# Attention and two feed-forward layers on one core: v's block sums on four quarters of TensorE's columns

## The chip, the cores and the metric

One core of a Trainium2 chip runs the whole kernel in one launch. Its engines are TensorE (matmul, PE in the profile, with its weight loads as PEld), VectorE (DVE), ScalarE (ACT), GpSimd (POOL) and SyncE (SP, which here issues every DMA). The metric is device time in microseconds of one execution; the median of several is compared.

## The reference, cut to what matters

```
# q, k, v: (2, 8, 768, 64) f32;  block 32, window 16
nb      = S // block                                   # 24 blocks
k_sum   = k.reshape(B, H, nb, block, D).max(axis=3)
v_sum   = v.reshape(B, H, nb, block, D).mean(axis=3)   # the sums that the change touches
scores  = [q k^T / 8 where |i - j| < 16 else -1e9,  q k_sum^T / 8 + log(32)]
a       = softmax(scores)                              # over 768 + 24 columns
attn    = a @ concat([v, v_sum])
x       = attn as (1536, 512)
h       = x @ w_in;  x = (h * cos(h)) @ w_out          # first feed-forward layer, 512 -> 2048 -> 512
...                                                    # second layer, solu and layer norm
```

## The kernel before

**Attention.** The 16 heads are taken as 8 pairs (n = 0 to 7), and the 768 queries of a pair as 12 tiles of 64, four tiles to a group, so three groups (g = 0, 1, 2) to a pair and 24 groups G. A query tile needs a window of 96 keys and the 24 block rows, 120 columns together. All engines follow one order written out by hand: `for step in range(29)` at the end of `attention()`. In a step TensorE makes the scores of group step+1 (`emit_s`, L561, tile `sps`), the transposes of the weights of group step-4 (`emit_t`, L598, `aps`) and the product with v of group step-5 (`emit_av`, L613, `ops`); where g is 2 it transposes k and q of pair n+2 (`emit_k` L494, `emit_q` L533). VectorE takes maxima and sums (L572, L585), GpSimd subtracts the maximum and multiplies by the reciprocal (L576, L591), ScalarE does the exponential (L581) and copies out of PSUM (`emit_kx`, `emit_kx_ends` with lines 522 and 525, `emit_qx` L547).

**v of a pair.** `load_v(n)` fills one of four buffers `vt` with the twelve overlapping windows: for each head one DMA of 240 KB (L440) and one of 48 KB (L444), in rows of 256 bytes. `sum_v(n)` (L472, tile `vsum`) sums blocks of 32 rows on TensorE: for each of twelve tiles one f32 matmul (two entries each in the trace) whose weights are 96 rows by 64 columns of ones and zeros from `strip`; tiles 0 to 5 add up in PSUM partitions 0 to 63 and tiles 6 to 11 in 64 to 127. `scale_v(n)` (L480) divides on ScalarE into `vm`. `place_vsum(n)` (L487) copies the 24 means behind the windows of all twelve tiles: two DMAs, each from 12 partitions of `vm` to 12 partitions of `vt`, every row written twelve times. The dictionaries `VSUM_AT` and `VLOAD_AT` say in which step pair n is summed and loaded; its placing is issued at the head of the step after its sum, and a load near the end of its step. `emit_av` of a pair's first group, in step 3n+5, needs the placed means.

**SP's order.** SP issues everything in the order of the program: loads of k and q (L408), of v, the placing, and the weights of the first layer (L141, tile `raw`, 512 KB each, eight in attention at the steps of `WSTEPS`). A weight tile then passes ScalarE (L162, L163), VectorE (L169), ScalarE and GpSimd (L186, L187).

**Fill.** The first four steps of the first layer (48 matmuls of 128x512, L277) are laid into attention's later steps: `FILL` says how many in which step. The first twelve add up in the one bank of pool `ps_h0`, which the sums of pairs 0 to 5 use before; the others need the banks of `ps_qk`, which are given over at step `QK_DONE`. Sums of pairs 6 and 7 stand in a `ps_qk` tile, between the k and q of two pairs. From the end of attention on, the two layers run (L277, L319, later L907, L1074).

```
VSUM_AT  = {1: 0, 5: 1, 8: 2, 10: 3, 13: 4, 14: 5, 16: 6, 19: 7}
VLOAD_AT = {1: 1, 4: 2, 6: 3, 8: 4, 10: 5, 13: 6, 16: 7}
```

Of the kernel before, what the change touches and what calls it, by code (L numbers as in the profile page):

```python
# [7 lines left out]
F32 = mybir.dt.float32  # L8
# [11 lines left out]
BAND = 16  # L20
QT = 64
WIN = 96
# [12 lines left out]
def fused_kernel(  # L35
# [15 lines left out]
    P = 128  # L51
    B, H, S, D = q.shape
# [4 lines left out]
    NT = S // QT  # L57
    NS = S // BLOCK
# [39 lines left out]
    DVE_X = 19  # L98
    DVE_NORM = 99
    LAST = 5  # L100
    QK_DONE = 20
    REBIAS = float(2.0 ** -112)
    NEGATIVE = float(2.0 ** 32)
    TOP3 = float(0.936 * 2.0 ** -29)
# [165 lines left out]
    def h_products(step):  # L270
        fg, tb, f = work[step]
        h = h_of[step] = h_tile(step)
        m = 0
        for c in range(KC):
            for (a, b_) in PASSES:
                w = weights.done[w1[fg][0][c]]
                nc.tensor.matmul(  # L277
                    h, lhsT=w[:, a, f * P:(f + 1) * P], rhs=xs_of[tb, c][:, b_, :],
                    start=(m == 0), stop=(m == 3 * KC - 1))
                m += 1  # L280
                yield
# [54 lines left out]
    ps_h0 = ps_stack.enter_context(tc.tile_pool(name="ps_h0", bufs=1, space=PSUM))  # L336
    qk_stack = ps_stack.enter_context(ExitStack())
    ps_qk = qk_stack.enter_context(tc.tile_pool(name="ps_qk", bufs=1, space=PSUM))
# [3 lines left out]
    def warm_up(n):  # L342

        if not n:
            return
        idle = idles[0]
        t = ps_h0.tile([P, 512], F32, tag="h", name="idle")
        for _ in range(n):
            nc.tensor.matmul(t, lhsT=idle[:, 0:P], rhs=idle, start=True, stop=True)


    FILL = {15: 3, 16: 3, 17: 3, 18: 3, 20: 4, 21: 4, 22: 4, 23: 4, 24: 4, 25: 4, 26: 4, 27: 4, 28: 4}
    early = (x for step in range(GF) for x in h_products(step))

    def fill(step):

        if step == QK_DONE:
            qk_stack.close()
            ps_h[0] = ps_stack.enter_context(tc.tile_pool(name="ps_h", bufs=3, space=PSUM))
        for _ in range(FILL.get(step, 0)):  # L360
            next(early, None)
# [23 lines left out]
    def attention():  # L385
        st = ExitStack()
        with st:
            io = st.enter_context(tc.tile_pool(name="io", bufs=2))
            fix = st.enter_context(tc.tile_pool(name="fix", bufs=1))
# [10 lines left out]
            q_t, k_t, v_t, kx_t, vs_t, qk_t, ks_t = {}, {}, {}, {}, {}, {}, {}  # L400
# [46 lines left out]
                    )  # L447
                v_t[n] = t

            HALF = NT // 2  # L450
            FIRST, FINAL, MID = 0, D, 2 * D
            strip = fix.tile([P, 3 * D + 2 * HALF], F32, name="strip")

            def block_columns():

                for at, row in ((FIRST, 0), (FINAL + 2 * HALF - 2, WIN - QT), (MID + 2 * HALF, BAND)):
                    nc.vector.tensor_reduce(
                        out=strip[:, at:at + 2],
                        in_=ident[:, row:row + QT].rearrange("p (b k) -> p b k", k=BLOCK), op=ALU.add, axis=AX.X)

            def blocks_of(t):
                at = FIRST if t == 0 else FINAL if t == NT - 1 else MID + 2 * HALF - 2 * (t % HALF)
                return strip[0:WIN, at:at + D]

            def sum_v(n):

                o = (ps_h0 if n < 6 else ps_qk).tile(
                    [P, 512] if n < 6 else [P, 2, 2, S // 2], F32, tag="h" if n < 6 else "qk", name="vsum")
                o = (o if n < 6 else o[:, 0, 0])[:, 0:P]
                for t in range(HALF):  # L470
                    for c in range(2):
                        nc.tensor.matmul(  # L472
                            o[D * c:D * c + D], lhsT=blocks_of(HALF * c + t),
                            rhs=v_t[n][0:WIN, HALF * c + t].rearrange("p j d -> p (j d)"),
                            start=(t == 0), stop=(t == HALF - 1))
                vs_t[n] = o

            def scale_v(n):
# [3 lines left out]

            def place_vsum(n):
                m = vs_t.pop(n)
                for c in range(2):
                    at = WIN + c * NS // 2
                    nc.sync.dma_start(  # L487
                        out=v_t[n][at:at + NS // 2].rearrange("p t j d -> p t (j d)"),
                        in_=m[D * c:D * c + NS // 2].unsqueeze(1).to_broadcast([NS // 2, NT, 2 * D]))

            def transposed(t, even, odd):

# [60 lines left out]
            def emit_s(G):  # L553
                n, g = divmod(G, GPP)
                qx, kx = kx_t["q", n], kx_t["k", n]
                sps = bank(G % 2, "sps").rearrange("p (i s) -> p i s", i=NG)[:, :, 0:KW]
                for i in range(NG):
                    t = NG * g + i
                    for j in range(2):
                        h = slice(D * j, D * j + D)  # L560
                        nc.tensor.matmul(  # L561
                            sps[h, i, :], lhsT=qx[h, t * QT:(t + 1) * QT], rhs=kx[h, t, :],
                            start=True, stop=True)
                ss_t[G] = sps
# [64 lines left out]
            NPAIR = B * NP  # L629
# [28 lines left out]

            LX, LN, LT, LA = 1, 2, 4, 5
            KX_FIRST = (1, 2, 3, 4, 5)  # L660
            VSUM_AT = {1: 0, 5: 1, 8: 2, 10: 3, 13: 4, 14: 5, 16: 6, 19: 7}
            VLOAD_AT = {1: 1, 4: 2, 6: 3, 8: 4, 10: 5, 13: 6, 16: 7}
            for step in range(NGR + LA):
                n, g = divmod(step, GPP)
                summed = LN <= step < NGR + LN
                ahead = 1 if step == 1 else n + 1 if g == 0 and 0 < n < NPAIR - 1 else 0

                warm_up(IDLE[g] if step < min(FILL) else 0)
                if step - 1 in VSUM_AT:
                    place_vsum(VSUM_AT[step - 1])  # L670
                if step + 1 < NGR:
                    emit_s(step + 1)
                if step == 0:
                    pair_k(1)
                    emit_max(0)
                    pair_q(1)
                    emit_k(1)
                    emit_q(1)
                if LT <= step < NGR + LT:
                    emit_t(step - LT)  # L680
                if g == 2 and n + 2 < NPAIR:
                    emit_k(n + 2)
                    emit_q(n + 2)
                fill(step)
                if step >= LA:
                    emit_av(step - LA)
                if step in VSUM_AT:
                    sum_v(VSUM_AT[step])

                if g == 1 and n in KX_FIRST:  # L690
                    emit_kx_ends(n + 1)
                if step == NGR:
                    emit_at(step - LT)
                if LX <= step < NGR + LX:
                    emit_exp(step - LX)
                weights.split()
                if 0 < step < NGR:
                    emit_max(step)
                if LT <= step < NGR + LT and step != NGR:
                    emit_at(step - LT)  # L700
                if g == 1 and 0 < n < NPAIR - 1 and n not in KX_FIRST:
                    emit_kx_ends(n + 1)
                if ahead:
                    emit_ksum(ahead)
                if summed:
                    emit_sum(step - LN)
                if step == NGR + 3:
                    emit_x(step - LA)
                weights.rebias()
                drain(step - NGR, 0)  # L710
                weights.finish()
                if summed:
                    emit_norm(step - LN)
                if step >= LA and step != NGR + 3:
                    emit_x(step - LA)
                drain(step - NGR, 1)
                if ahead:
                    emit_kx(ahead)
                if step == 1:
                    emit_kx_ends(1)  # L720
                    emit_qx(1)
                if g == 2 and n + 2 < NPAIR:
                    emit_qx(n + 2)
                if step == 2:
                    weights.load(0)
                if step in WSTEPS:
                    weights.bits()
                for c in range(KC):
                    if step == XS[c]:
                        xs_of[0, c] = split_x(0, c, xs_a)  # L730
                if g == 1 and n + 2 < NPAIR:
                    pair_k(n + 2)
                    pair_q(n + 2)

                if g == 1 and n + 3 < NPAIR:
                    load_k(n + 3)
                    load_q(n + 3)
                if step in VLOAD_AT:
                    load_v(VLOAD_AT[step])
                if step in VSUM_AT:  # L740
                    scale_v(VSUM_AT[step])

# [682 lines left out]
```

## Time and profile before

| | us |
|---|---|
| three runs | 477.5, 479.46, 482.5 |
| their median | 479.46 |
| the profiled execution | 477.52 |
| its span, first to last instruction | 475.7 |
| TensorE busy in the span | 467.1 (98%) |

The profiled execution is 1.8 us longer than its span and 1.9 us under the median. The granted clock of TensorE is 1.000 in it. Times in the rows below are microseconds from the start of the span. Attention reaches to the first matmul of L319, at 97.17 us, and two layers follow.

### The profile page before, as it was taken

To read this page: it belongs to the slowest core of one execution; us is meant where nothing else is said; L and a number is where in the kernel's file an instruction comes from. 1 tells how busy PE (TensorE), PEld (TensorE's weight loads), DVE (VectorE), ACT (ScalarE), POOL (GpSimd) and SP (SyncE) were. 2 spreads that over 40 slices of the span, in tenths; PEclk is the share of its full clock that TensorE was granted. 3 is DMA by queue.
4 is the path that set the end of the run, shared out by engine and by line. 5 is a ranking of instruction groups with operands and counts; after the bars stand their busy time and mean duration, and the time that the engine had idled before them with its cause. 6 is when DMAs were issued, how large, how long until landed. Compare 5 with 4: busy or idle time off the path is not lost.

```text
span 475.7 us, 8064 instructions
## 1 busy us (share of the span) xinstructions
PE 467.1 (98%) x2899; PEld 384.2 (81%) x2899; DVE 317.6 (67%) x754; ACT 314.4 (66%) x558; POOL 227.3 (48%) x230
## 2 busy tenths in 40 slices
PE   8999999999999999999999999999999999999997
PEld 4788877788888888888888888888888888888886
DVE  3989965663554456566464647474799999988930
ACT  3689888757675866556665456664872448888891
POOL 2689988424322222222223723655105878795450
PEclk9999999999999999999999999999999999999999
DMA  7999875001223222233222122110210031436351
GB/s 210 269 230 248 219 182 177 12 1 45 90 95 116 99 88 90 90 113 108 90 88 88 45 88 87 49 45 1 88 45 1 22 84 28 119 59 113 88 133 68
DMA packets 61304, 46.52 MB, mean 98 GB/s; under 512 B 42704, under 2 KB 53712, under 8 KB 61264
## 3 DMA queue, kind: packets, MB, share of 16 engines
q1 hardware_dynamic: 61264, 46.01, 34.3%
q8 instruction: 23, 0.38, 0.3%
q14 instruction: 17, 0.14, 0.1%
HBM read 36.43 MB, written 3.15 MB: 83 GB/s over the span
## 4 chain that ended last, share of the span: by engine, by line
PE 88%; POOL 4%; DVE 3%; DMA 2%; ACT 1%; issue 1%; SPq 0%; DVEq 0%; POOLq 0%
PE y L319 27%; PE h L277 27%; PE h L1074 14%; PE h L907 12%; PE sps L561 2%; PE ops L613 2%; PE aps L598 1%; POOL sm L576 1%; PE vsum L472 1%; POOL sm L591 1%; DMA qt<-in_q_dram 1%; DMA raw<-in_moe_w_out_dram 1%; POOL w L187 1%; DVE sm L572 1%; DVE ksum L506 1%
## 5 line engine op out<-in xcount | busy, mean ns | idle before, releaser
L277 PE MATMUL h<-xs,w 128*128 128x512 f32 x576 | 141.2, 391 | 0.0
L319 PE MATMUL y<-gs,w 128*128 128x512 f32 x576 | 138.2, 389 | 0.0
L319 PEld LDWEIGHTS y<-gs,w 128*128 128x128 f32 x576 | 108.0, 188 | 22.4
L277 PEld LDWEIGHTS h<-xs,w 128*128 128x128 f32 x576 | 107.2, 188 | 21.6
L187 POOL TENSOR_TENSOR w<-s,w 128x512 fp32r<-128x512 f32 x32 | 41.7, 1303 | 97.1 <-ACT w L186 95.1
L286 ACT ACTIVATE r<-h 128x512 int32<-128x512 f32 x48 | 28.6, 597 | 87.1 <-PE h L277 87.1
L291 DVE SCALAR_TENSOR_TENSOR r<-r,h 128x512 f32<-128x512 int32 x48 | 32.9, 686 | 71.0 <-ACT r L286 70.8
L1074 PE MATMUL h<-w,ls 128*128 128x512 f32 (+1 forms) x312 | 66.8, 374 | 0.0
L169 DVE SCALAR_TENSOR_TENSOR s<-raw 128x512 int32<-128x512 int32 x48 | 37.7, 786 | 40.5 <-ACT raw L163 39.2
L1074 PEld LDWEIGHTS h<-w,ls 128*128 128x128 f32 x312 | 55.3, 188 | 10.9 <-POOL ls L1051 0.6
L907 PE MATMUL h<-w,xo 128*128 128x512 f32 x252 | 58.7, 390 | 0.0
L907 PEld LDWEIGHTS h<-w,xo 128*128 128x128 f32 x252 | 47.1, 188 | 9.7
L296 ACT ACTIVATE r<-r,half_pi 128x512 f32<-128x512 f32 x48 | 34.5, 720 | 5.4 <-DVE r L291 5.3
L307 DVE TENSOR_TENSOR gs<-h,gs 128x512 fp32r<-128x512 f32 x48 | 32.6, 680 | 5.3 <-ACT gs L306 5.3
L301 DVE TENSOR_TENSOR h<-h,r 128x512 f32<-128x512 f32 x48 | 33.0, 688 | 4.0 <-ACT r L296 3.9
L162 ACT ACTIVATE raw<-raw 128x512 f32<-128x512 f32 x48 | 32.0, 667 | 1.0 <-DMA raw<-in_moe_w_out_dram 1.0
L778 POOL TENSOR_TENSOR w<-s,w 128x512 fp32r<-128x512 f32 x14 | 17.9, 1294 | 30.9 <-ACT w L777 30.9
L163 ACT ACTIVATE raw<-raw 128x512 int32<-128x512 uint32 x48 | 32.0, 666 | 0.0
L576 POOL TENSOR_TENSOR sm<-sm,mx 128x480 f32<-128x480 f32 x24 | 24.7, 1031 | 8.7 <-DVE mx L572 8.7
L306 ACT ACTIVATE gs<-h 128x512 fp32r<-128x512 f32 x48 | 28.2, 587 | 0.4 <-DVE h L301 0.3
L1044 ACT ACTIVATE s<-turned 128x1024 uint16<-128x1024 uint16 x20 | 26.5, 1367 | 2.3 <-POOL xo L895 1.8
L591 POOL TENSOR_TENSOR sm<-sm,ss 128x480 f32<-128x480 f32 x24 | 27.2, 1134 | 1.4 <-DVE ss L586 1.3
(105 smaller groups left out, 667.8 us busy)
## 6 DMA issues: line engine op xcount, KB each, us to landing
raw<-in_moe_w_in_dram SPq DMA_DIRECT2D x24, 512.0 KB, 3.7
raw<-in_moe_w_out_dram SPq DMA_DIRECT2D x24, 512.0 KB, 3.4
vt<-in_v_dram SPq DMA_DIRECT2D x16, 240.0 KB, 5.3
kt<-in_k_dram SPq DMA_DIRECT2D x8, 384.0 KB, 3.2
qt<-in_q_dram SPq DMA_DIRECT2D x8, 384.0 KB, 7.8
out_dram<-osb SPq DMA_DIRECT2D x11, 256.0 KB, 2.1
vt<-vm SPq DMA_DIRECT2D x16, 72.0 KB
vt<-in_v_dram SPq DMA_DIRECT2D x16, 48.0 KB, 6.0
```

The source lines that it names most:

```text
L162: nc.scalar.activation(out=hw, in_=hw, func=AF.Prelu, scale=REBIAS, alpha=NEGATIVE)
L163: nc.scalar.activation(out=lw, in_=lw.bitcast(U32), func=AF.Copy, scale=TOP3)
L169: nc.vector.scalar_tensor_tensor(out=self.f32[i], in0=t[:, :, 1], scalar=3, in1=t[:, :, 0], op0=ALU.logical_shift_left, op1=ALU.bitwise_or)
L187: nc.gpsimd.tensor_tensor(out=w[:, 1, :], in0=f, in1=as32(w[:, 0, :]), op=ALU.subtract)
L277: nc.tensor.matmul(h, lhsT=w[:, a, f * P:(f + 1) * P], rhs=xs_of[tb, c][:, b_, :], start=(m == 0), stop=(m == 3 * KC - 1))
L291: nc.vector.scalar_tensor_tensor(out=r, in0=r.bitcast(I32), scalar=TWO_PI, in1=h_of[step], op0=ALU.mult, op1=ALU.subtract)
L296: nc.scalar.activation(out=r, in_=r, func=AF.Sin, scale=-1.0, bias=half_pi)
L301: nc.vector.tensor_tensor(out=h, in0=h, in1=r, op=ALU.mult)
L307: nc.vector.tensor_tensor(out=gs[:, 1, :], in0=r, in1=as32(gs[:, 0, :]), op=ALU.subtract)
L319: nc.tensor.matmul(y[e], lhsT=w[:, a, e * P:(e + 1) * P], rhs=gs[:, b_, :], start=(f == 0 and i == 0), stop=(f == GF - 1 and i == 2))
L907: nc.tensor.matmul(banks_of[p][BANK[m]], lhsT=x[:, a, s0:s0 + P], rhs=w2_of[m, c][:, b_, :], start=c == j == 0, stop=c == 1 and j == 2)
L1074: nc.tensor.matmul(o, lhsT=ls_of[t][f // 4][:, a, s0:s0 + P], rhs=w[:, b_, cols], start=(f == 0 and i == 0), stop=(f == NF2 - 1 and i == 2))
```

## The change

It makes the block sums of v on four quarters of TensorE's columns where there were two halves: weights of 32 columns, three tiles to a quarter, output in PSUM partitions 32c to 32c+5. The number of matmuls stays at twelve for a pair. `place_vsum` becomes four DMAs of 6 partitions where there were two of 12. Pairs 4, 5 and 7 are summed in steps 12, 15 and 20 (before 13, 14 and 19); pair 6 stays in step 16 but uses `ps_h0`. Pairs 4 and 5 are loaded one step later (9 and 11), behind the placing of pairs 2 and 3 in SP's order; with pair 4's sum in step 12 its placing stands ahead of the loads of step 13, pair 6's among them. Fill leaves steps 15, 16 and 20 and goes to 17, 18 and 21 to 24; `QK_DONE` is 21. Block maxima and the key copy of pair 2 move from step 3 to step 2.

```diff
-    QK_DONE = 20
+    QK_DONE = 21
...
-    FILL = {15: 3, 16: 3, 17: 3, 18: 3, 20: 4, 21: 4, 22: 4, 23: 4, 24: 4, 25: 4, 26: 4, 27: 4, 28: 4}
+    FILL = {17: 6, 18: 6, 21: 5, 22: 5, 23: 5, 24: 5, 25: 4, 26: 4, 27: 4, 28: 4}
...
-            HALF = NT // 2
-            FIRST, FINAL, MID = 0, D, 2 * D
-            strip = fix.tile([P, 3 * D + 2 * HALF], F32, name="strip")
+            QUARTER, NQ = NT // 4, 32
+            FIRST, FINAL, MID = 0, NQ, 2 * NQ
+            strip = fix.tile([P, 3 * NQ + 2 * QUARTER], F32, name="strip")
...
-                at = FIRST if t == 0 else FINAL if t == NT - 1 else MID + 2 * HALF - 2 * (t % HALF)
-                return strip[0:WIN, at:at + D]
+                at = FIRST if t == 0 else FINAL if t == NT - 1 else MID + 2 * QUARTER - 2 * (t % QUARTER)
+                return strip[0:WIN, at:at + NQ]
...
-                o = (ps_h0 if n < 6 else ps_qk).tile(
-                    [P, 512] if n < 6 else [P, 2, 2, S // 2], F32, tag="h" if n < 6 else "qk", name="vsum")
-                o = (o if n < 6 else o[:, 0, 0])[:, 0:P]
-                for t in range(HALF):
-                    for c in range(2):
+                o = (ps_h0 if n < 7 else ps_qk).tile(
+                    [P, 512] if n < 7 else [P, 2, 2, S // 2], F32, tag="h" if n < 7 else "qk", name="vsum")
+                o = (o if n < 7 else o[:, 0, 0])[:, 0:P]
+                for t in range(QUARTER):
+                    for c in range(4):
                         nc.tensor.matmul(
-                            o[D * c:D * c + D], lhsT=blocks_of(HALF * c + t),
-                            rhs=v_t[n][0:WIN, HALF * c + t].rearrange("p j d -> p (j d)"),
-                            start=(t == 0), stop=(t == HALF - 1))
+                            o[NQ * c:NQ * c + NQ], lhsT=blocks_of(QUARTER * c + t),
+                            rhs=v_t[n][0:WIN, QUARTER * c + t].rearrange("p j d -> p (j d)"),
+                            start=(t == 0), stop=(t == QUARTER - 1), tile_position=(0, NQ * c))
...
-                for c in range(2):
-                    at = WIN + c * NS // 2
+                for c in range(4):
+                    at = WIN + c * NS // 4
                     nc.sync.dma_start(
-                        out=v_t[n][at:at + NS // 2].rearrange("p t j d -> p t (j d)"),
-                        in_=m[D * c:D * c + NS // 2].unsqueeze(1).to_broadcast([NS // 2, NT, 2 * D]))
+                        out=v_t[n][at:at + NS // 4].rearrange("p t j d -> p t (j d)"),
+                        in_=m[NQ * c:NQ * c + NS // 4].unsqueeze(1).to_broadcast([NS // 4, NT, 2 * D]))
...
-            VSUM_AT = {1: 0, 5: 1, 8: 2, 10: 3, 13: 4, 14: 5, 16: 6, 19: 7}
-            VLOAD_AT = {1: 1, 4: 2, 6: 3, 8: 4, 10: 5, 13: 6, 16: 7}
+            VSUM_AT = {1: 0, 5: 1, 8: 2, 10: 3, 12: 4, 15: 5, 16: 6, 20: 7}
+            VLOAD_AT = {1: 1, 4: 2, 6: 3, 9: 4, 11: 5, 13: 6, 16: 7}
...
-                ahead = 1 if step == 1 else n + 1 if g == 0 and 0 < n < NPAIR - 1 else 0
+                ahead = step if step in (1, 2) else n + 1 if g == 0 and 1 < n < NPAIR - 1 else 0
```

## Rows read from the trace of the kernel before

**Rows 1.** Busy time by stretch: PE, PEld, DVE, ACT, POOL, clock, DMA share, GB/s.
```profile
24.00:38.00 14.00, 13.84 (x224) 11.87 (x226) 12.30 (x55) 11.97 (x26) 12.00 (x11) 1.00 0.95 245
38.00:52.00 14.00, 14.00 (x232) 11.97 (x227) 13.76 (x49) 12.83 (x29) 13.51 (x13) 1.00 0.84 204
52.00:64.00 12.00, 11.93 (x177) 10.02 (x176) 7.82 (x36) 10.46 (x23) 10.24 (x10) 1.00 0.84 203
64.00:74.00 10.00, 8.75 (x119) 6.93 (x119) 7.72 (x33) 8.12 (x17) 9.01 (x9) 1.00 0.77 217
```

**Rows 2.** The chain that ended last, 10 to 100 us: start, duration, what.
```profile
13.86 1.46 PE vsum L472 x24
...
22.85 1.27 DVE qg L426
...
25.04 0.61 PE ops L613 x16
25.65 1.31 PE vsum L472 x24
...
34.77 1.31 PE vsum L472 x24
...
62.13 3.92 DMA raw<-in_moe_w_out_dram
...
66.08 0.67 ACT raw L162
...
73.51 1.60 PE vsum L472 x24
...
76.66 0.94 PE h L277 x4
...
97.17 2.94 PE y L319 x12
```

**Rows 3.** SP's timeline, 49 to 76 us: start, duration, what it issues.
```profile
52.67 0.41 SPq L440 DMA_DIRECT2D vt<-in_v_dram  x1
...
55.98 2.13 SPq L444 DMA_DIRECT2D vt<-in_v_dram  x1
58.22 3.80 SPq L487 DMA_DIRECT2D vt<-vm  x4
62.13 0.96 SPq L141 DMA_DIRECT2D raw<-in_moe_w_out_dram  x2
...
75.45 1.64 SPq L487 DMA_DIRECT2D vt<-vm  x2
```

**Rows 4.** Busy time of two stretches, columns as in rows 1.
```profile
76.80:78.90 2.10, 2.10 (x34) 1.62 (x34) 0.74 (x3) 2.07 (x5) 2.10 (x3) 1.00 0.68 71
...
47.00:49.00 2.00, 2.00 (x38) 1.60 (x34) 1.97 (x8) 2.00 (x5) 1.58 (x2) 1.00 1.17 286
```

**Rows 5.** What SP's queue waited for, 17 to 62 us: total, times, longest.
```profile
SPq L487 <- ACT qx L547: 1.3, 1, 1.3
SPq L487 <- ACT kx L525: 0.8, 2, 0.4
SPq L487 <- ACT sm L581: 0.7, 1, 0.7
```

**Rows 6.** DMA issues of the page: KB each, median us from issue to landing.
```profile
vt<-in_v_dram SPq DMA_DIRECT2D x16, 240.0 KB, 5.3
```

**Rows 7.** TensorE's timeline, 57 to 76 us, with idle time and what ended it.
```profile
61.34 1.48 PE L472 MATMUL vsum<-vt,strip 96*64 96x128 f32 x24
62.75 1.04 PE L561 MATMUL sps<-kx,qx 64*64 64x120 f32 x16
...
65.46 0.88 PE L533 MATMUL qk<-ident,qg 128*128 128x128 f32 x6 [0.44 <-DVE qg L426]
...
73.51 1.60 PE L472 MATMUL vsum<-vt,strip 96*64 96x128 f32 x24 [0.81 <-ACT kx L522]
```

More of the change, by code (lines that the diff above doesn't have):

```diff
@@ L448, in load_v @@
                 v_t[n] = t
-            HALF = NT // 2
-            FIRST, FINAL, MID = 0, D, 2 * D
-            strip = fix.tile([P, 3 * D + 2 * HALF], F32, name="strip")
+            QUARTER, NQ = NT // 4, 32
+            FIRST, FINAL, MID = 0, NQ, 2 * NQ
+            strip = fix.tile([P, 3 * NQ + 2 * QUARTER], F32, name="strip")
             def block_columns():
-                for at, row in ((FIRST, 0), (FINAL + 2 * HALF - 2, WIN - QT), (MID + 2 * HALF, BAND)):
+                for at, row in ((FIRST, 0), (FINAL + 2 * QUARTER - 2, WIN - QT), (MID + 2 * QUARTER, BAND)):
                     nc.vector.tensor_reduce(
```

## The prediction

> **What bounds the kernel now.** I read the busy time by stretch first [rows 1]. The diff touches attention alone, up to 97.17 us; what follows is TensorE end to end and only moves with that point. From 24 to 64 us TensorE is busy nearly all the time, so a shorter sum looks like time won. But the DMA share stands at 0.95, 0.84 and 0.84 in the same stretches, and VectorE and GpSimd are at 13.8 and 13.5 of 14 us from 38 to 52. Three things are full at once.
>
> The chain of waits [rows 2] says which of them decides where. A sum of v stands on it four times, at 13.86, 25.65, 34.77 and 73.51. Behind the first comes VectorE's copy of q at 22.85, so what the first sum saves is lost there. Between 38 and 73 the chain runs over other engines, and at 62.13 over a weight load of 3.92 us on which ScalarE starts at 66.08. That load was issued late: SP's timeline [rows 3] shows it right behind four placing DMAs (3.80 us), and these behind the loads of pair 6's v, whose last issue at 55.98 held SP for 2.13 us. Attention's second half is paced by this queue as much as by TensorE.
>
> **The sums themselves.** 24 entries take 1.31 us [rows 2]: twelve times 0.109 us with two halves side by side. Four quarters abreast would be six times that, 0.65 us. The densest packing that the trace shows is `ops`, 16 entries in 0.61 us or 38 ns each [rows 2], and 24 at that rate are 0.91 us, which I take. A sum then saves 0.40 us, at best 0.65, nothing if quarters overlap no better than halves, and it loses 1.3 if they run one after another. On the chain that is three sums, 1.2 us (up to 2.0).
>
> **The placing.** It goes from two DMAs a pair to four of half the size. SP needs 0.82 us for each now, with an empty queue at 75.45 (1.64 for two), and 0.95 where four stand in a row. Size does not set that: a load of 240 KB at 52.67 takes SP 0.41 us [rows 3], a placing of 72 KB twice as long. So a DMA of 6 partitions lies between 0.41 (half) and 0.95, and I take 0.82, its nearest row.
>
> The transfers say the same. While placing runs nearly alone, from 76.8 to 78.9, the DMA share is 0.68 at 71 GB/s; where v is loaded it is 1.17 at 286 GB/s [rows 4]. Two placings are 147 KB, so about 2.1 us, 1.04 us each. A share of 0.68 is some 11 of 16 engines, so a DMA over 12 partitions seems to keep at most 12 engines busy, and one over 6 might keep 6. The page DMA: Bandwidth & Descriptors of the Trainium skill, in its section Why a DMA increments its semaphore by 16 and not by 1, says that the number of engines is the largest up to 16 that divides the slowest dimension, and that they are the lowest-numbered ones. By that rule the trace agrees for 12 partitions (0.68 is under 12/16), the four new DMAs would queue on the same six engines, and placing would take 4.2 us a pair however fast SP issues it: 12 x 1.04 = 12.5 us in place of the 9.8 below.
>
> **Where that is paid.** The load of pair 6 stays in step 13 and its sum in step 16, but what SP has ahead of it changes: now the placing of pairs 0 to 3 (8 DMAs), then of pairs 0 to 4 (20), since pair 4's sum moves to step 12. That is 12 x 0.82 = 9.8 us more in the queue (20 x 0.41 - 8 x 0.82 = 1.6 to 20 x 0.95 - 8 x 0.82 = 12.4). Some is absorbed: SP's placing waits for ScalarE 1.3 + 0.8 + 0.7 = 2.8 us between 17 and 62 [rows 5], and a later SP finds these done. Net 7.0.
>
> Pair 6's second large load is issued just ahead of 55.98 and such loads land after 5.3 us [rows 6], at about 60.8; TensorE begins that sum at 61.34 without waiting [rows 7]. There is half a microsecond to spare. Seven more puts the landing at 67.8, the sum's end at 68.7 where it is 62.75 now: +5.95 us. TensorE takes instructions in order, so the scores and transposes of step 17, and VectorE, GpSimd and ScalarE behind them, wait with it. What TensorE saved earlier is spent in this wait.
>
> From that sum to 97.17 there are 34.4 us now. Behind it come six more fill matmuls (steps 15 and 16 lose theirs, 17 and 18 double): 6 x 0.235 = 1.4 us, from four in 0.94 [rows 2]. The last sum shrinks from 1.60 to 0.91 and its wait of 0.81 for `emit_kx_ends` goes, as it moves a step back; the wait of 0.44 for q goes too [rows 7]. Together -0.5. The weight load of step 18 now stands behind two more pairs' placing (another 3.3 us); nearest row for what that costs is ScalarE's wait before 66.08, under a microsecond; I take +0.5. The other loads that were moved behind placing (pairs 4 and 5) are needed three or four steps later, and those of k and q are wanted earlier than pair 6's v: they may wait too, but inside the same 7 us. Moving pair 2's maxima a step forward changes the order of VectorE's work, not its amount: nothing, and up to half a microsecond either way if the copy of q at 22.85 shifts. The smaller `strip` and its memset lie in the first 10 us under loads: nothing.
>
> Sum: 5.95 - 0.5 + 0.5 = +6.0 us. The profiled execution was 477.5, which gives 483.5. It lies 1.9 under the median of the runs; to be compared with that median, 479.46 + 6 = **485.4**.
>
> **Rivals.** *Half the size, half the time.* Quarter DMAs cost 0.41 each. Then the queue grows by 1.6 us less what is absorbed, and the sum of pair 6 ends between 60.9 and 63.3: -2.3 to 0 us, 477 to 479.5. For it: each DMA has half the packets. Against: SP's time did not follow size. It decides whether the landing of pair 6's v moves at all.
>
> *The other side, faster: loads arrive in time.* If quarter placings run side by side and take less than now, v of pair 6 is there when TensorE comes, and its saving reaches the end: 1.2 to 2.0 for sums, 1.25 for two waits, and near 1.0 for ScalarE's wait before 66.08, since only half as many placings of pairs 4 and 5 then precede that load. That is -3.5 to -4.3, 475 to 476. For it: TensorE at 14.00 of 14 us [rows 1]. It decides if landing comes before about 60 us. The same page's section Rules for kernel authors holds that transfers to separate partition halves gain nothing, as they share engines; nothing here has shown four together other than the row of 3.80 us.
>
> *The quarters do not overlap.* 24 entries of 0.109 one by one are 2.6 us a sum. Two sums behind pair 6's landing would cost 3 more than forecast: 488.5. The halves' overlap speaks against it.
>
> **Chances and range.** Forecast (482.5 to 488, its end from 12.4 us of queue): 0.60. Half the time: 0.23. Faster: 0.12. No overlap: 0.05. What a measurement of this kernel tells from no change is about 1%, 4.8 us. Slower by more: seven tenths of the forecast and the last case, 0.47. Faster by more: only the far end of the third, 0.05. The rest, 0.48, within. 477 to 489 leaves out most of the third case and a thin end above.
>
> **What would show it.** Right: SP takes some 3.3 us for a pair's four placings; TensorE has a wait of several us before the sum of pair 6, ended by a DMA on `vt`; a sum takes 0.65 to 0.91 us; the first L319 matmul lies near 103. Wrong: placings of 0.4 us, a DMA share while placing as high as now, no wait at that sum, and L319 at 97 or before. The prediction fails above all if a placing's cost follows its size.

## The result, and the profile after

The changed kernel takes 484.03 us (median of 13 runs, 482.04 to 486.93) where the kernel before takes 479.46 (13 runs beside them, 477.5 to 482.5). The ratio is 1.0102, 95% interval 1.0078 to 1.0125: slower by about 1%. The forecast was 485.4. The profiled execution of after took 483.99 us with a span of 482.2, 6.5 us more than the span before.

Busy time by stretch first, columns as in [rows 1]; the last line is a stretch in which little but placing moves data, and answers to [rows 4].

```profile
24.00:38.00 14.00, 12.82 (x212) 10.22 (x210) 13.49 (x56) 12.13 (x25) 11.78 (x11) 1.00 0.78 202
38.00:52.00 14.00, 13.87 (x242) 11.41 (x242) 12.48 (x48) 13.37 (x30) 13.89 (x13) 1.00 0.88 240
52.00:64.00 12.00, 7.42 (x124) 5.89 (x124) 9.08 (x36) 9.43 (x20) 10.25 (x10) 1.00 0.73 194
64.00:74.00 10.00, 8.26 (x82) 7.00 (x84) 4.36 (x20) 3.11 (x7) 4.05 (x4) 0.66 0.76 193
...
85.90:89.60 3.70, 3.70 (x45) 2.63 (x43) 2.91 (x18) 2.17 (x5) 3.70 (x5) 1.00 0.32 39
```

From 52 to 64 TensorE is busy for 7.42 of 12 us, where it had 11.93 [rows 1]. In the next stretch the granted clock is 0.66, where it was 1.00. So there are two things to find: what TensorE waited for, and what that did to its clock. TensorE's timeline of after has both (start, duration, what; in brackets the idle time ahead and what ended it):

```profile
35.05 0.69 PE L613 MATMUL ops<-at,vt 120*64 120x64 f32 x16 [0.80 <-DMA vt<-vm]
...
59.13 0.69 PE L613 MATMUL ops<-at,vt 120*64 120x64 f32 x16
65.74 1.63 PE L472 MATMUL vsum<-vt,strip 96*32 96x128 f32 x24 [5.92 <-DMA vt<-in_v_dram]
67.29 1.87 PE L561 MATMUL sps<-kx,qx 64*64 64x120 f32 x16
69.09 1.11 PE L598 MATMUL aps<-ident,sm 128*120 128x128 f32 x4
...
103.03 5.73 PE L319 MATMUL y<-gs,w 128*128 128x512 f32 x24
```

The 5.92 us ahead of 65.74 are the wait for pair 6's v; the same sum began at 61.34 with no wait in the kernel before [rows 7]. Behind the idle stretch the same instructions take nearly twice as long: scores 1.87 us against 1.04 at 62.75 in [rows 7]. The granted clock is 0.50 from 65.7 to 70.0 and 1.00 again from 72 on. The chain of waits of after says what stood behind that load, and where the first sum's gain went:

```profile
23.29 1.27 DVE qg L426
24.55 0.04 issue
24.60 0.88 PE qk L533 x6
25.47 0.61 PE ops L613 x16
26.09 0.79 PE vsum L472 x24
...
31.79 3.01 DMA vt<-vm
34.80 0.25 issue
35.05 0.69 PE ops L613 x16
...
61.23 0.45 SPq L440
61.68 0.04 issue
61.72 3.88 DMA vt<-in_v_dram
```

The first sum is shorter, but TensorE still waits for VectorE's copy of q at 23.29 (22.85 in [rows 2]). At 35.05 it stands 0.80 us for a placing, a wait that [rows 2] do not have. Pair 6's v lands at 61.72 + 3.88 = 65.60. SP's timeline shows why that load left late, and one row grouped by tile gives SP's time for each placing (count, then ns as least, median and most):

```profile
45.79 3.06 SPq L487 DMA_DIRECT2D vt<-vm  x4
...
52.65 3.90 SPq L487 DMA_DIRECT2D vt<-vm  x4
...
58.35 1.21 SPq L440 DMA_DIRECT2D vt<-in_v_dram  x1
...
61.72 1.87 SPq L444 DMA_DIRECT2D vt<-in_v_dram  x1
```

```profile
L487 SPq DMA_DIRECT2D vt<-vm x32: 720/722/1198, 16.6 to 87.2; - x32
```

The four placings of pair 4 (52.65 to 56.55) now stand ahead of the loads of step 13, and pair 6's large loads are issued at 58.35 and 61.23. Before they were issued at 52.67 [rows 3] and 55.50:

```profile
55.50 0.44 SPq L440 DMA_DIRECT2D vt<-in_v_dram  x1
```

So the second one is issued 5.7 us later. Each placing costs SP 0.72 us though it moves half as much.

### The profile page after: what moved, and what is told of

It is laid out like the page before. It is cut to its first block, busy times and chain, and to the rows that moved or that the text cites. A ratio compares the mean times of both kernels' runs of the same rounds, so it can differ in the third digit from the quotient of the medians.

```text
span 482.2 us, 8091 instructions
## 1 busy us (share of the span) xinstructions
PE 465.7 (97%) x2899; PEld 381.5 (79%) x2899; DVE 319.6 (66%) x754; ACT 313.9 (65%) x558; POOL 226.6 (47%) x230
## 4 chain that ended last, share of the span: by engine, by line
PE 88%; DVE 4%; DMA 2%; issue 1%; ACT 1%; SPq 1%; POOL 1%; POOLq 0%; ACTq 0%
PE h L277 27%; PE y L319 27%; PE h L907 12%; PE h L1074 10%; PE sps L561 3%; PE ops L613 3%; PE aps L598 2%; PE vsum L472 1%; DMA qt<-in_q_dram 1%; DMA vt<-in_v_dram 1%; PE qk L533 1%; DMA vt<-vm 1%; DVE qg L426 1%; PE qk L494 1%; DVE bn L969 0%
## 5 line engine op out<-in xcount | busy, mean ns | idle before, releaser
L319 PE MATMUL y<-gs,w 128*128 128x512 f32 x576 | 138.2, 389 | 0.0
L319 PEld LDWEIGHTS y<-gs,w 128*128 128x128 f32 x576 | 108.0, 188 | 22.5
L561 PE MATMUL sps<-kx,qx 64*64 64x120 f32 x384 | 25.5, 274 | 3.0 <-DVE mx L572 1.7
```

The costliest lines, as they stand in the source:

```text
L319: nc.tensor.matmul(y[e], lhsT=w[:, a, e * P:(e + 1) * P], rhs=gs[:, b_, :], start=(f == 0 and i == 0), stop=(f == GF - 1 and i == 2))
L561: nc.tensor.matmul(sps[h, i, :], lhsT=qx[h, t * QT:(t + 1) * QT], rhs=kx[h, t, :], start=True, stop=True)
```

## The experiments

All were timed beside the kernel before, whose medians there were 478.05 to 478.81 us; the ratio is against that. Where an edit adds lines, those behind it have other numbers: a placing stands in L487, L488 or L502, a sum in L472 or L477.

### The parts: order alone, quarters alone, placings alone

The kernel before with the new order of sums, loads, fill and maxima alone; sums stay on halves, with two placings a pair:

```diff
-    QK_DONE = 20
+    QK_DONE = 21
...
-    FILL = {15: 3, 16: 3, 17: 3, 18: 3, 20: 4, 21: 4, 22: 4, 23: 4, 24: 4, 25: 4, 26: 4, 27: 4, 28: 4}
+    FILL = {17: 6, 18: 6, 21: 5, 22: 5, 23: 5, 24: 5, 25: 4, 26: 4, 27: 4, 28: 4}
...
-            VSUM_AT = {1: 0, 5: 1, 8: 2, 10: 3, 13: 4, 14: 5, 16: 6, 19: 7}
-            VLOAD_AT = {1: 1, 4: 2, 6: 3, 8: 4, 10: 5, 13: 6, 16: 7}
+            VSUM_AT = {1: 0, 5: 1, 8: 2, 10: 3, 12: 4, 15: 5, 16: 6, 20: 7}
+            VLOAD_AT = {1: 1, 4: 2, 6: 3, 9: 4, 11: 5, 13: 6, 16: 7}
...
```

The edits that move pair 6's sum to `ps_h0` and pair 2's maxima to step 2 are those of the change.

> The new order of sums, loads and fill, with sums on halves and two placing DMAs a pair as before. Queue theory (SP's time for placing ahead of pair 6's v makes the stall): ten placings of 0.83 us stand ahead of that load where before had eight, so it lands near 62 and TensorE waits about 2 us at that sum, with no fall of its clock: 479 to 481 us, ratio 1.000 to 1.004. Order theory (moving sums, loads and fill is what costs, whatever the form): as the changed kernel, 484, ratio 1.010.

The reverse, the kernel before with the change's `strip`, `blocks_of`, `sum_v` loops and `place_vsum`, in the old order:

```diff
-                for t in range(HALF):
-                    for c in range(2):
+                for t in range(QUARTER):
+                    for c in range(4):
...
-                for c in range(2):
-                    at = WIN + c * NS // 2
+                for c in range(4):
+                    at = WIN + c * NS // 4
...
```

> Quarters and four placing DMAs alone, with the old order, loads and fill. Queue theory: sixteen placings of 0.77 us stand ahead of pair 6's v where there were eight of 0.83, 5.7 us more of which some 2 is absorbed; it lands near 64, TensorE waits about 3 us at that sum: 481 to 483 us, ratio 1.003 to 1.008. Order theory: no stall, the sums' half microseconds come through: 477 to 479, ratio 0.995 to 1.000.

And the kernel before with its sums untouched and nothing but four placings of 6 partitions in place of two of 12:

```diff
-                for c in range(2):
-                    at = WIN + c * NS // 2
+                for c in range(4):
+                    at = WIN + c * NS // 4
+                    row = D * (c // 2) + NS // 4 * (c % 2)
...
-                        in_=m[D * c:D * c + NS // 2].unsqueeze(1).to_broadcast([NS // 2, NT, 2 * D]))
+                        in_=m[row:row + NS // 4].unsqueeze(1).to_broadcast([NS // 4, NT, 2 * D]))
```

> The kernel before with one edit: each pair's means are placed in four DMAs of 6 partitions; sums stay on halves. Queue theory: the stall of the run with quarters in the old order, or half a microsecond more, since sums are not shorter: 481 to 484 us, ratio 1.004 to 1.010, and DMA share of a placing alone near half of 0.68. If it is the matmuls on quarters that cost, this is the kernel before: ratio 1.000.

| kernel | median us | ratio, 95% |
|---|---|---|
| new order, halves, two placings | 479.57 | 1.0032 [1.0010, 1.0055] |
| old order, quarters, four placings | 488.0 | 1.0198 [1.0152, 1.0245] |
| old order, halves, four placings | 486.54 | 1.0162 [1.0124, 1.0199] |
| the change, from above: new order, quarters, four placings | 484.03 | 1.0102 [1.0078, 1.0125] |

Four placings instead of two cost the old order 1.6% with the sums left alone. Adding the quarter sums does not change that by more than the intervals. So the loss is the placing's, and the new order gives part of it back: with four placings it is worth about 1 of the 2%. Both kernels in the old order are slower than was expected of them (481 to 484 us). The wait was expected at pair 6's sum, and in the traces that sum waits 0.22 us with quarters and not at all with halves; where the time goes is shown below. The first kernel's chain and TensorE's timeline show the queue at work with two placings a pair:

```profile
56.42 5.60 DMA vt<-in_v_dram
```

```profile
62.15 1.62 PE L472 MATMUL vsum<-vt,strip 96*64 96x128 f32 x24 [1.46 <-DMA vt<-in_v_dram]
```

Pair 6's v lands at 62.02, 3.6 us earlier than in the changed kernel whose order it shares. Its pairs 0 to 4 put 10 placings of 0.79 ahead of that load, the change 20 of 0.72: 6.5 us more in the queue, of which 3.6 reach the landing. In the old order the wait moves to the users of the means. TensorE's timelines, with quarters and then with halves:

```profile
38.38 1.12 PE L613 MATMUL ops<-at,vt 120*64 120x64 f32 x16 [3.25 <-DMA vt<-vm]
...
61.39 0.69 PE L613 MATMUL ops<-at,vt 120*64 120x64 f32 x16 [1.43 <-DMA vt<-vm]
```

```profile
49.25 0.68 PE L614 MATMUL ops<-at,vt 120*64 120x64 f32 x16 [2.70 <-DMA vt<-vm]
```

Nothing was added to TensorE there; it stands for the placing itself, and with quarters its first L319 matmul begins at 109.17. In the changed kernel, whose loads of pairs 4 and 5 stand behind the placing, the one wait of this kind is 0.80 us at 35.05.

### Is it SP's time or the transfer?

In the kernel before, four placings of 12 partitions and six tiles each: as many DMAs and bytes as with 6 partitions, on twice as many partitions each.

```diff
-                for c in range(2):
-                    at = WIN + c * NS // 2
+                for c in range(4):
+                    at = WIN + c // 2 * NS // 2
+                    tiles = slice(c % 2 * NT // 2, (c % 2 + 1) * NT // 2)
...
-                        out=v_t[n][at:at + NS // 2].rearrange("p t j d -> p t (j d)"),
+                        out=v_t[n][at:at + NS // 2, tiles].rearrange("p t j d -> p t (j d)"),
...
```

> The kernel before with each pair's means placed in four DMAs, but cut by tiles and not by partitions: 12 partitions and 6 of the 12 tiles each. As many DMAs and packets as in the run with four placings of 6 partitions (ratio 1.016), whose only difference is on how many partitions a DMA lies. If SP's issue time is the cost: some 0.75 us each again, ratio 1.012 to 1.020. If it is the transfers, which crowd on half as many engines there: as many engines as before stay busy, ratio 1.000 to 1.005, with SP's time still doubled.

It took 489.18 us, ratio 1.0212 [1.0162, 1.0263]: no better than the 1.0162 of 6 partitions. In the chain of this kernel a placing lands 2.33 us after its issue, in the one with 6 partitions after 2.94 (one landing each, of different pairs). Then SP's time for a placing in this kernel, grouped by tile, and a stretch in which little but four placings moves data, columns as in [rows 1]:

```profile
32.70 2.33 DMA vt<-vm
```

```profile
L488 SPq DMA_DIRECT2D vt<-vm x32: 778/779/1512, 17.0 to 91.0; - x32
```

```profile
89.50:92.50 3.00, 3.00 (x42) 2.42 (x40) 0.42 (x1) 2.26 (x6) 2.89 (x3) 1.00 0.26 38
```

A transfer that lands 0.6 us sooner did not help. What both kernels share is SP's four issues of over 0.7 us a pair, and the data moves at that pace: 38 GB/s here, 39 in the change, 71 with two placings of twice the size [rows 4].

The same DMAs issued from ScalarE's queue in the changed kernel:

```diff
-                    nc.sync.dma_start(
+                    nc.scalar.dma_start(
```

> The changed kernel with its four placings issued from ScalarE's queue and not SP's. If SP's issue time is the cost, pair 6's v is issued some 12 us of queue earlier and lands before TensorE comes; but each issue takes some 0.75 us of ScalarE, 3 us a pair, which is busy 12 to 13 of 14 us: 482 to 488. If the transfers on few engines are the cost, v still lands late, TensorE still waits several us at that sum: over 486.

503.5 us, ratio 1.0503 [1.0442, 1.0564], far slower than I had priced it. ScalarE's timeline:

```profile
60.78 4.53 ACTq L487 DMA_DIRECT2D vt<-vm  x4
65.35 0.34 ACT L522 ACTIVATE kx<-qk 128x192 f32<-128x192 f32 x1 [4.60 <-DMA vt<-vm]
```

An issue costs ScalarE about as much as SP (median 0.75 us), and the next step of ScalarE's order stands behind all four: 4.60 us here. The 32 issues are 24 us of an engine that is busy 12.1 and 13.4 of 14 us in the stretches of after, and the kernel is 19.5 us slower than the change. I had counted as if ScalarE had room. No engine waits for a load of v in this kernel, as the queue theory had said; but TensorE comes to pair 6's sum 11 us later than in the change, so that decides little.

### Moving the load out of the queue's way, and the clock

Pair 4's sum back in step 13, so that its placing stands behind the load of pair 6:

```diff
-            VSUM_AT = {1: 0, 5: 1, 8: 2, 10: 3, 12: 4, 15: 5, 16: 6, 20: 7}
+            VSUM_AT = {1: 0, 5: 1, 8: 2, 10: 3, 13: 4, 15: 5, 16: 6, 20: 7}
```

> The changed kernel with pair 4's sum back in step 13, so that its four placings stand behind the load of pair 6's v and not ahead of it. Queue theory: that load is issued 3 us earlier, lands near 62.5, TensorE waits 2 to 3 us where it waited 5.9, and its clock does not fall (2.4 us more): 478 to 481 us, ratio 0.998 to 1.003. Order theory and quarters theory: nearly the same order and the same sums, 484, ratio 1.010.

480.58 us, ratio 1.0045 [1.0022, 1.0067]. One number moved, and more than half of the loss is gone; the time lies in the queue theory's range, the ratio somewhat above it. TensorE's timeline:

```profile
61.86 1.20 PE L472 MATMUL vsum<-vt,strip 96*32 96x128 f32 x24 [2.48 <-DMA vt<-in_v_dram]
62.99 1.87 PE L561 MATMUL sps<-kx,qx 64*64 64x120 f32 x16
```

The wait is 2.48 us instead of 5.92 and the sum begins 3.9 us earlier; the four placings that no longer stand ahead are 3.90 us in SP's timeline of after. The clock fell all the same, which was not expected: the scores take 1.87 us again, and the granted clock is 0.79 from 62 to 70.

For the clock, matmuls on a tile that nobody reads (26 of them in the trace), ahead of pair 6's sum in the changed kernel:

```diff
+                if step == 16:
+                    warm_up(27)
```

> The changed kernel with 27 matmuls of 128x512 bf16 on a tile of zeros right before pair 6's sum (some 5.8 us of TensorE time into a bank that is then free; nothing reads them). Clock theory: they fill the wait, v lands when it did, near 65.6, and the 2.4 us by which the sum and the next six groups ran longer at a granted clock near half are won back: 481 to 482 us, ratio 1.003 to 1.006. If the fallen clock costs nothing at the end: 484, ratio 1.010; if the filling itself delays the sum, over 485.

```profile
60.55 6.00 PE L349 MATMUL idle<-idle 128*128 128x512 bf16 x26
67.19 0.98 PE L472 MATMUL vsum<-vt,strip 96*32 96x128 f32 x24 [0.64 <-DMA vt<-in_v_dram]
```

The granted clock stays at 1.00 and the sum takes 0.98 us instead of 1.63. From that sum's end to L319 there are 34.1 us (102.23 - 68.17), where after has 35.7 (103.03 - 67.37): the fallen clock costs some 1.6 us behind the sum and 0.65 in it. The time, 483.06 us and 1.0094 [1.0061, 1.0126], cannot be told from after's 1.0102; in this profile the load landed 1.4 us later (59.79 + 7.26 = 67.05), which would hide most of the gain. The load was issued earlier there (59.30, in after 61.23). That landing is one profile's, and what made it later is open. So the clock's part is seen in the rows and not proved in the time.

Pair 6's sum one step later, with six fills moved too:

```diff
-    FILL = {17: 6, 18: 6, 21: 5, 22: 5, 23: 5, 24: 5, 25: 4, 26: 4, 27: 4, 28: 4}
+    FILL = {18: 6, 19: 6, 21: 5, 22: 5, 23: 5, 24: 5, 25: 4, 26: 4, 27: 4, 28: 4}
...
-            VSUM_AT = {1: 0, 5: 1, 8: 2, 10: 3, 12: 4, 15: 5, 16: 6, 20: 7}
+            VSUM_AT = {1: 0, 5: 1, 8: 2, 10: 3, 12: 4, 15: 5, 17: 6, 20: 7}
```

> The changed kernel with pair 6's sum one step later (17) and the first twelve fill matmuls in steps 18 and 19. Queue theory: the landing near 65.6 stays, but step 17's scores, transposes and product (3.5 us) run while v is on its way, so the wait is about 2 us and the clock stays: 478 to 480 us, ratio 0.997 to 1.002. If the loss lies in the placing's transfers or in the sums and not in this one wait: 483 to 485, ratio 1.008 to 1.011.

482.22 us, 1.0074 [1.0045, 1.0103], a smaller gain than hoped. TensorE and VectorE in their timelines:

```profile
64.86 1.54 PE L494 MATMUL qk<-ident,kg 128*128 128x128 f32 x6 [3.09 <-DVE kg L426]
```

```profile
62.14 1.12 DVE L169 SCALAR_TENSOR_TENSOR s<-raw 128x512 int32<-128x512 int32 x1 [2.49 <-ACT raw L163]
```

The wait for v became a wait for VectorE's copy of k, and behind that the granted clock is 0.50 from 64 to 70, where it had been expected to stay. That copy stands in VectorE's order behind a weight's `s`, and `s` waits for ScalarE.

### One placing for a pair

To have the quarter sums without their four DMAs: a matmul picks the 24 rows of `vm` out of four quarters into 24 adjacent partitions, ScalarE copies them, and one DMA places them, two steps after the sum. `QK_DONE` becomes 22.

```diff
+                nc.tensor.matmul(
+                    o[0:NS], lhsT=pick,
+                    rhs=m, start=True, stop=True)
...
+                nc.scalar.activation(out=m[0:NS], in_=o[0:NS], func=AF.Copy)
...
-                for c in range(4):
...
+                nc.sync.dma_start(
+                    out=v_t[n][WIN:WIN + NS].rearrange("p t j d -> p t (j d)"),
+                    in_=m[0:NS].unsqueeze(1).to_broadcast([NS, NT, 2 * D]))
...
-    FILL = {17: 6, 18: 6, 21: 5, 22: 5, 23: 5, 24: 5, 25: 4, 26: 4, 27: 4, 28: 4}
+    FILL = {18: 6, 19: 6, 22: 6, 23: 6, 24: 6, 25: 6, 26: 4, 27: 4, 28: 4}
...
-            VSUM_AT = {1: 0, 5: 1, 8: 2, 10: 3, 12: 4, 15: 5, 16: 6, 20: 7}
+            VSUM_AT = {1: 0, 5: 1, 8: 2, 10: 3, 12: 4, 14: 5, 16: 6, 20: 7}
```

> Sums on quarters, then one more f32 matmul a pair that gathers the 24 rows into partitions 0 to 23 (24 columns picked from the identity), one more copy on ScalarE, and one placing DMA of 24 partitions; placed two steps after the sum, pair 5's sum in step 14, fill in steps 18, 19 and from 22 on. Queue theory: five placings of 0.8 us stand ahead of pair 6's v where the kernel before has eight, TensorE pays 0.8 + 0.2 us a sum where it paid 1.3, ScalarE 0.3 us more a pair: no wait of several us at pair 6's sum, 475 to 479 us, ratio 0.993 to 1.000. If something other than the queue holds attention, 480 or more.

481.22 us, 1.0047 [1.0024, 1.0070]: the gain is less than expected. The wait for pair 6's v is gone from TensorE's timeline, and again VectorE's copy of k behind a weight's `s` stands in its place. Grouped by tile, the placing in this kernel; then TensorE and VectorE in their timelines:

```profile
L502 SPq DMA_DIRECT2D vt<-vg x8: 821/827/1012, 20.5 to 84.4; - x8
```

```profile
66.14 0.88 PE L509 MATMUL qk<-ident,kg 128*128 128x128 f32 x6 [2.00 <-DVE kg L426]
```

```profile
63.44 1.10 DVE L169 SCALAR_TENSOR_TENSOR s<-raw 128x512 int32<-128x512 int32 x1 [2.51 <-ACT raw L163]
```

One placing of 144 KB takes SP 0.83 us, a quarter of it 0.72. The wait in VectorE's timeline pointed to the weights. In this kernel, and in the one with pair 4's sum in step 13, I moved the conversions of steps 15 and 16:

```diff
-    WSTEPS = (4, 7, 10, 13, 15, 16, 18, 19)
+    WSTEPS = (4, 7, 10, 13, 17, 18, 19, 20)
```

> One gathered placing, with the weight conversions of steps 15 and 16 moved to 17 to 20. In the run with the gathered placing VectorE stood 2.5 us before 63.44 for a weight's bits from ScalarE, its copy of k came 1 us behind that, and TensorE waited 2.0 us for the copy before its transposes at 66.14. If that order of the weights is what is late next once the queue is relieved, VectorE's wait and TensorE's 2.0 us go, the clock stays up, and the time is 478 to 479.5 us, level with the kernel before. If ScalarE as a whole is what is late (it makes four more copies of the gathered means), the same work comes back in steps 17 to 20 and the time stays at 481.

> The changed kernel with pair 4's sum back in step 13, and the same move of the weight conversions from steps 15 and 16 to 17 to 20. The loads of pair 6's v stand ahead of the moved weights in SP's queue and don't feel it, so by the queue theory TensorE still waits about 2.5 us for that v and the time stays at 480 to 481 us. If it is the weights' conversion on ScalarE and VectorE that holds the second half, the time falls to 479 or below.

> The kernel before with nothing but the weight conversions of steps 15 and 16 moved to 17 to 20: the control for the run with one gathered placing and the same move, which came out level with the kernel before. If that run is level because the move by itself takes something off any order, this one falls to about 475 to 477 us. If the move only mends what the changed order and its gather had made late, this one stays at 478 to 480, or loses up to 1 us because three weights then crowd the steps 18 to 20.

| kernel, all with weights later | median us | ratio, 95% |
|---|---|---|
| one gathered placing | 478.21 | 0.9983 [0.9963, 1.0003] |
| four placings, pair 4's sum in step 13 | 483.2 | 1.0093 [1.0060, 1.0127] |
| the kernel before (control) | 478.21 | 0.9998 [0.9972, 1.0025] |

With one placing the wait goes and the kernel is level with the one before, as its expectation said; the control shows that the move by itself is worth nothing. With four placings the same move costs: 480.58 became 483.2, which neither theory had. SP's and ScalarE's timelines of that kernel:

```profile
60.00 6.18 SPq L487 DMA_DIRECT2D vt<-vm  x8
```

```profile
65.47 0.28 ACT L480 ACTIVATE vm<-vsum 128x128 f32<-128x128 f32 x1 [3.22 <-DMA vt<-vm]
...
77.08 0.65 ACT L162 ACTIVATE raw<-raw 128x512 f32<-128x512 f32 x1 [2.04 <-DMA raw<-in_moe_w_out_dram]
```

Without the weight load between them, eight placings stand in a row. ScalarE's wait of 3.22 us for a placing to release `vm` is not what the move added: with the weights in their old place it is 3.72. New is the wait of 2.04 us for a weight, issued behind all twelve placings at 72.39. TensorE then waits for ScalarE's copy of `X`, and its clock falls (the granted clock is 0.77 from 80 to 90):

```profile
78.59 1.12 PE L613 MATMUL ops<-at,vt 120*64 120x64 f32 x16 [1.88 <-ACT X L627]
```

This fits the queue theory: I had looked at pair 6's v alone and not at who else stands behind placings. It is read from one profile and was not tested by a run of its own.

No version beat the kernel before. Why the gathered one is only level can be counted from TensorE's timelines: a sum of 0.86 us and a gather of 0.40 are 1.26, against 1.48 for a sum on halves [rows 7]. Eight times 0.22 is 1.8 us of TensorE's time at the most; its first L319 matmul begins at 96.94, in the same view of the kernel before at 97.11. Where the rest of the 1.8 goes was not followed.

## Why the prediction was right, step by step

**The sums** were taken at 0.91 us, at best 0.65; they take 0.79 in the chain, 33 ns an entry. That the first one's gain would be lost behind VectorE's copy of q is what the chain of after shows at 23.29. The rival without overlap (2.6 us a sum) is out.

**The placing** was taken at 0.82 us for a DMA of half the size. It is 0.72, nearer to 0.82 than to 0.41, and the rival of half the size for half the time (0.41) is out. SP's four median values stand in one line: 0.72 for 36 KB of 6 partitions, 0.78 for 36 KB of 12, 0.81 for 72 KB of 12 (0.82 at 75.45 in [rows 3]) and 0.83 for 144 KB of 24. Four times the bytes cost 15% more.

**The engines under it.** While four placings go, the DMA share is 0.32 at 39 GB/s, where two had 0.68 at 71 [rows 4]. The prediction read such a share as a count of engines. The Trainium skill's page DMA: Bandwidth & Descriptors, section Why a DMA increments its semaphore by 16 and not by 1, gives 6 engines to a DMA over 6 partitions. A share under 6/16 does not contradict that, but no run here shows it: with 12 partitions and six tiles the share is 0.26 at 38 GB/s, no higher. Share and rate are what transfers at the pace of SP's issues would give. What the prediction left as an alternative, that transfers on few engines would set the queue's pace and not SP, is out by the same kernel: it is no faster.

**The queue** was put at 12 x 0.82 = 9.8 us less 2.8 absorbed, net 7.0. With the median times it is 20 x 0.72 - 8 x 0.81 = 7.9; with the gaps and the few longer ones the placings ahead of that load hold SP for 16.4 us, before 7.2, so 9.2 more. The load's issue came 5.7 us later, and it landed 4.4 us behind that, where 5.3 had been taken: at 65.60, which is 4.8 later than the 60.8 estimated for before. The amount absorbed was near, its cause was another. Of the 2.8 us of waits for ScalarE in [rows 5], 0.7 lies at 60, behind the load; ahead of it such waits are 2.1 us before and 1.7 after. What became shorter is SP's time for the eleven small loads of v (L444) from pair 1's on: 17.2 us, before 20.4. Why these hold SP less was not tested. The sum's end was forecast at 68.7 and came at 67.37.

**The part behind it** is the step that failed. I had -0.5 for the last sum and the vanished waits and +0.5 for the weight load, no change in all. From the sum's end to L319 there are 35.7 us instead of 34.4. The reason in the rows is the clock: behind 5.92 us of idle time it is 0.66 over ten microseconds (a mean of 0.50, that is 1.2 GHz, up to 70.0 and of the full 2.4 GHz from 72 on), which I had not put into the sum at all, neither for pair 6's sum itself (1.63 us instead of 0.79) nor for what follows. The kernel with the idle matmuls has 34.1 us there at a clock of 1.00, as the forecast wanted. Two small terms were wrong as well and cancel in part. The wait of 0.81 us for `emit_kx_ends` did not go, it moved from the last sum to the scores ahead of it:

```profile
80.35 1.04 PE L561 MATMUL sps<-kx,qx 64*64 64x120 f32 x16 [0.76 <-ACT kx L525]
```

And ScalarE waits for no weight load behind pair 6's sum, for which the forecast had +0.5; its one such wait near it, 1.12 us, ends at 61.37.

**The total** is right partly by luck. L319 was forecast near 103 and begins at 103.03, since a landing 2.2 us too late in the forecast and some 2.3 us of slow clock not in it cancel. The profiled execution rose by 6.47 us for a forecast of 6.0; the median by 4.6, since the profiled execution of before lay 1.9 under its median and that of after on its own.

**The faster rival** needed the landing before about 60. It stays wrong for four placings in any order tried. One placing came nearest, where the sum of pair 6 waits only 0.26 us once the weights are out of the way, and there the gather eats most of the gain. That the order itself is nearly free (1.0032) was not in my rivals: I had blamed the move of pair 4's sum and the number of DMAs together, and the runs show that the move costs little with two placings a pair and over half of the loss with four.

## What to carry to other kernels

Count the DMAs and not only the bytes when one engine issues all of them: splitting these small copies into twice as many cost the issuing queue nearly double, and what was issued behind them moved by a good part of that (5.7 of 9.2 us at pair 6's load). Before a matmul is made denser, see what its output's new layout does to the copies that read it. And a wait on TensorE is to be priced with what the clock does behind it.

## What was not expected of the hardware

- SP's time for a placing follows neither bytes nor partitions much (0.72 to 0.83 us from 36 to 144 KB), while it issues a load of 240 KB in 0.41 [rows 3]. What in these copies makes their issue dear was not tried.
- ScalarE pays 0.75 us for the same issue, and its next step stands behind it.
- After one idle stretch of 5.92 us TensorE's granted clock is 0.66 over the stretch from 64 to 74, in a kernel whose mean is 0.993.
- Twenty-four f32 entries of 128 columns on four column quarters take 0.79 us, on two halves 1.31 [rows 2]: 1.66 times as fast and not twice.
